# Merging weight bits in PSUM, and shorter chains of small operations, in an attention, memory and MLP kernel

## The chip, the cores and the metric

The kernel runs on one core of a Trainium2 chip. The time is what the device takes for one launch, in microseconds (us). The engines are TensorE (PE: matrix products and transposes, with PEld for its weight loads), VectorE (DVE), ScalarE (ACT), GpSimd (POOL) and SyncE (SP), whose queue starts the transfers (DMA). PSUM is the memory that PE writes to; SBUF is the large on-chip memory.

## The reference

Attention with a memory term over 4 batches, 8 heads, 576 positions of 64 values, then two matrix products over all 2304 tokens with a gate between them:

```python
scores = q @ k.T / sqrt(64), causal
a = exp(scores - max);  a /= a.sum(-1) + 1e-09;  local = a @ v
q_p = phi(q)                                  # max(q,0) + exp(min(q,0))
mem_out = (q_p @ M_prev) / ((q_p * z_prev).sum(-1) + 1e-6)
g = 1 / (1 + exp(-beta))                      # one value a head
x = g * mem_out + (1 - g) * local             # 2304 x 512
h = x @ w_in;  h = h / (1 + exp(-1.702 * h));  out = h @ w_out
```

`w_in` (512 x 2048) and `w_out` (2048 x 512) come as float64 and are used at float32 precision. Each float32 operand is used as a high and a low float32r part, and a product is the sum of three partial products.

## The kernel before

**Weights.** Both matrices are cut into 16 blocks of 128 x 512 values. A block arrives as pairs of 32-bit words (`wraw`, 512 KB). `conv_unit` makes float32 of it: ACT scales the upper words (L148), and DVE does three operations on bits in the SBUF tile `wr`: a shift (L153), the sign by and/or (L154), the low word by shift/or (L156). Then ACT copies the high part (`wi` or `wo`, L90), and POOL subtracts to get the low part (L100). Raw tiles: two buffers for `w_in`, three for `w_out`.

**Stages.** `first_queries` does the first 256 positions of batch 0 for all four head pairs. Then 16 (batch, head pair) units called pairs run through attention, one every 7 or 8 slots. `plan_prep` splits inputs into parts, computes phi(q) (`qm`, `qp`), its norm (`nrm`) and the memory matrix parts `ms`; `plan_attend` computes scores into PSUM tiles `ps`, maxima (L452), exponentials with sums (L458, `a` and `at`, sums in `sm` and `st`), inverses (L498 and L499, L526 and L528), scaling on POOL (L461), transposes (`pt`), their parts (`e`), and products with v into `po`. The result of a pair is `xf`, stored to DRAM (`xd`) and read back in chunks of x (`xl`, `xh`). The first matmul (`first_moe`, PSUM tiles `pm`, later `pm2`) runs over 8 chunks of tokens times 16 blocks and fills PE between attention work; its results `hk` go to DRAM (`gd`), copied out of PSUM by DVE and ACT in turn. The second stage reads them back (`graw`), gates them (`gt`, `gh`, `gl`) and multiplies by `w_out` (`acc`).

**The norm of the memory term.** The minimum of q with 0 is a DVE operation (L388), the exponential is ACT's (L392). DVE reduces over 64 values (L406), adds 1e-6 (L408), inverts (L409) and multiplies by the gate (L100, `nrm<-nrm,g`). `ms` is a copy (L93) and a subtraction (L100) of the memory matrix on DVE.

**What sets the order.** The program is written as events in slots; the framework then puts every engine's instructions into one list by its own schedule, which each engine follows. Pools hand out their buffers in the order of the program: a tile waits for the buffer's earlier tile, whatever the lists say. `ps_s` has five PSUM buffers under the tag "ps" for `ps` and `pt`; `ps_m2` has six for `pm2` in the late stage. In the program the 16 `w_in` conversions stand behind `first_queries` and ahead of all pairs; those of `w_out` are handed out one every two slots near the end of the first matmul.

Of the kernel before, what the change touches and what calls it, by code (L numbers as in the profile page):

```python
# [34 lines left out]
def tile_attention_memory_moe(ctx, tc, kq, vq, mem, zz, beta, w_in, w_out, out):  # L35
# [151 lines left out]
    def first_queries(b):  # L187
        K = []
# [50 lines left out]
        def phi():  # L239
            nc.vector.tensor_scalar(out=qm, in0=q, scalar1=0.0, scalar2=None, op0=ALU.min)  # L240
            nc.scalar.activation(out=qm, in_=qm, func=AF.Exp)
            nc.vector.scalar_tensor_tensor(out=q, in0=q, scalar=0.0, in1=qm, op0=ALU.max, op1=ALU.add)
            for c in range(NP):
                tt("P", qm[:, c], q[:, c], z[:, c:c + 1, :].to_broadcast([128, 2, 128]), ALU.mult)

        def phin():
            n = fst.tile([128, NP, 2, 2, 1], F32, name="fn")
            nc.vector.tensor_reduce(
                out=n[:, :, :, :, 0], in_=qm.rearrange("p c t (h d) -> p c t h d", h=2), op=ALU.add, axis=AX.X)
            nc.vector.tensor_scalar(out=n, in0=n, scalar1=1e-6, scalar2=None, op0=ALU.add)  # L250
# [1 line left out]
            for t in range(2):
                w = n[:, :, t, :, 0]
                tt("V", w, w, g.rearrange("p (c h) -> p c h", h=2), ALU.mult)
# [596 lines left out]
```

## Time and profile before

| | us |
|---|---|
| median of 3 runs | 706.65 (706.03 to 709.79) |
| the profiled execution | 706.16 |
| its span | 703.7 |

| engine | busy us in the span | share |
|---|---|---|
| PE | 632.4 | 90% |
| DVE | 493.9 | 70% |
| ACT | 393.4 | 56% |
| POOL | 292.3 | 42% |

The profiled execution lies within the runs; 2.5 us of its time lie outside the span. The mean granted clock of PE is 0.973. The shares are averages over stages that differ: conversions and the first pairs up to some 100 us, pairs with the first matmul to some 420 us, the end of the first matmul with the `w_out` conversions to 502.6 us, then the second matmul. So the profile is read by stretches of time, and in each by the chain of waits, which is followed back from the last instruction of the stretch to what released it. What stands in that chain ends last; a busy engine that is not in it can be shortened without effect.

### The profile page before, as it was taken

The numbers are of one execution on the slowest core, as the hardware profiler recorded it, in microseconds if no ns is written. First come the engines' busy times: TensorE is split into PE (matmuls) and PEld (weight loads), VectorE is DVE, ScalarE is ACT, GpSimd is POOL, SyncE is SP. The second block draws the span as 40 slices with busy tenths as digits, with TensorE's granted clock in tenths as the row PEclk, the third lists the DMA queues.
The fourth block names the chain that finished last, engine by engine and source line by source line (L and its number), as shares of the span: only waits on it lengthen the run. The fifth ranks groups of instructions, "written<-read, shape, count | busy, mean of one in ns | idle before, by whom it ended". The sixth has DMA issues, their size and how long they took to land.

```text
span 703.7 us, 12530 instructions
## 1 busy us (share of the span) xinstructions
PE 632.4 (90%) x3984; PEld 575.1 (82%) x3984; DVE 493.9 (70%) x1194; ACT 393.4 (56%) x951; POOL 292.3 (42%) x303
## 2 busy tenths in 40 slices
PE   3468887879998889999899999878999999999997
PEld 2256776669997789999899999778988888888897
DVE  4999998898778886687767635997255555555453
ACT  4467566686657764667576533543244545444453
POOL 4878766688447791665575203454000000000000
PEclk9989998999999999999999999999999999999999
DMA  8657858786677665766772128875233435335241
GB/s 257 181 193 198 243 153 227 197 234 170 174 203 195 187 196 174 198 173 175 231 195 82 44 85 308 277 214 186 83 90 105 150 104 152 100 101 151 69 128 53
DMA packets 71425, 116.70 MB, mean 166 GB/s; under 512 B 8768, under 2 KB 41024, under 8 KB 71360
## 3 DMA queue, kind: packets, MB, share of 16 engines
q1 hardware_dynamic: 71360, 115.91, 56.1%
q8 instruction: 32, 0.52, 0.3%
q14 instruction: 33, 0.27, 0.1%
HBM read 63.97 MB, written 27.79 MB: 130 GB/s over the span
## 4 chain that ended last, share of the span: by engine, by line
PE 62%; DVE 20%; DMA 7%; issue 4%; ACT 4%; SPq 1%; POOL 1%; DVEq 0%; ACTq 0%; POOLq 0%
PE acc L81 28%; PE pm L81 17%; PE po L81 6%; PE pt L85 5%; PE ps L81 4%; DVE wr L154 3%; DVE ps L452 3%; DVE wr L156 2%; DMA wraw<-in_w_in_dram 2%; DVE e L100 1%; DVE wr L153 1%; DMA gd<-hk 1%; DVE ms L93 1%; DMA graw<-gd 1%; DVE sm L498 1%
## 5 line engine op out<-in xcount | busy, mean ns | idle before, releaser
L81 PE MATMUL pm<-xh,wi 128*128 128x288 f32 (+2 forms) x1024 | 221.3, 306 | 13.4 <-ACT hk L90 7.1
L81 PEld LDWEIGHTS pm<-xh,wi 128*128 128x128 f32 x1024 | 168.9, 193 | 18.3 <-ACT hk L90 8.7
L81 PE MATMUL acc<-gh,wo 128*128 128x512 f32 (+1 forms) x640 | 179.7, 368 | 0.0
L81 PE MATMUL pm<-xl,wi 128*128 128x288 f32 (+2 forms) x512 | 153.7, 303 | 0.0
L81 PEld LDWEIGHTS acc<-gh,wo 128*128 128x128 f32 x640 | 115.2, 189 | 19.8
L81 PE MATMUL acc<-gl,wo 128*128 128x512 f32 (+1 forms) x320 | 115.5, 368 | 0.0
L461 POOL TENSOR_SCALAR a<-a,sm,g 128x512 f32<-128x512 f32 (+3 forms) x112 | 74.5, 677 | 59.6 <-DVE sm L499 32.8
L81 PEld LDWEIGHTS pm<-xl,wi 128*128 128x128 f32 x512 | 98.6, 193 | 0.3
L100 DVE TENSOR_TENSOR e<-pt,e 128x320 fp32r<-128x320 f32 (+2 forms) x152 | 69.5, 480 | 23.1 <-ACT e L90 22.4
L752 DVE SCALAR_TENSOR_TENSOR gt<-gt,graw 128x512 f32<-128x512 f32 (+1 forms) x80 | 52.1, 652 | 46.7 <-ACT gt L751 46.4
L100 DVE TENSOR_TENSOR gl<-gt,gh 128x512 fp32r<-128x512 f32 (+1 forms) x80 | 52.0, 650 | 46.0 <-ACT gh L90 42.9
L458 ACT ACTIVATE a<-ps,nm 128x512 f32<-128x512 f32 (+3 forms) x112 | 60.5, 542 | 36.8 <-DVE nm L452 34.1
L452 DVE CUSTOM_DVE_ANT_0 ps<-ps,mask 128x256 f32<-128x256 f32 (+4 forms) x144 | 69.3, 494 | 15.5 <-PE ps L81 10.9
L81 PE MATMUL po<-e,vs 128*128 128x320 f32 (+3 forms) x416 | 73.3, 295 | 4.1 <-DVE e L100 3.1
L90 ACT ACTIVATE e<-pt 128x320 fp32r<-128x320 f32 (+2 forms) x152 | 61.3, 433 | 27.3 <-PE pt L85 14.1
L751 ACT ACTIVATE gt<-graw 128x512 f32<-128x512 f32 (+1 forms) x80 | 47.1, 590 | 51.6 <-DVE gl L100 51.6
L90 ACT ACTIVATE gh<-gt 128x512 fp32r<-128x512 f32 (+1 forms) x80 | 47.1, 589 | 49.9 <-PE acc L81 46.6
L81 PEld LDWEIGHTS po<-e,vs 128*128 128x128 f32 x416 | 63.6, 195 | 6.1 <-DVE e L100 4.2
L81 PEld LDWEIGHTS acc<-gl,wo 128*128 128x128 f32 x320 | 59.4, 189 | 10.0
L81 PE MATMUL ps<-W 128*128 128x512 f32 (+3 forms) x224 | 59.1, 350 | 6.8 <-ACT at L458 1.8
L85 PE MATMUL pt<-ident,a 128*128 128x128 f32 x296 | 58.7, 282 | 1.4 <-ACT a L458 0.6
L85 PE MATMUL pt<-ident,at 128*128 128x128 f32 x160 | 43.0, 292 | 8.4 <-DVE e L100 5.0
(118 smaller groups left out, 1016.1 us busy)
## 6 DMA issues: line engine op xcount, KB each, us to landing
graw<-gd SPq DMA_DIRECT2D x64, 256.0 KB, 2.6
gd<-hk SPq DMA_DIRECT2D x96, 144.0 KB, 2.5
wraw<-in_w_in_dram SPq DMA_DIRECT2D x16, 512.0 KB, 4.0
wraw<-in_w_out_dram SPq DMA_DIRECT2D x16, 512.0 KB, 4.8
kqr<-in_kq_dram SPq DMA_DIRECT2D x12, 608.0 KB, 5.2
W<-hi SPq DMA_DIRECT2D x24, 272.0 KB, 4.0
W<-loq SPq DMA_DIRECT2D x48, 128.0 KB, 3.6
vr<-in_vq_dram SPq DMA_DIRECT2D x16, 320.0 KB, 4.0
```

What stands on the lines that cost most here:

```text
L81: nc.tensor.matmul(out, l, r, start=start, stop=stop)
L85: nc.tensor.transpose(out, in_, idn)
L90: nc.scalar.activation(out=dst, in_=src, func=AF.Copy, **kw)
L93: nc.vector.tensor_copy(dst, src)
L100: (nc.vector if eng == "V" else nc.gpsimd).tensor_tensor(out=dst, in0=a, in1=b, op=op)
L154: nc.vector.scalar_tensor_tensor(out=ri, in0=raw[:, :, 1], scalar=-2 ** 31, in1=ri, op0=ALU.bitwise_and, op1=ALU.bitwise_or)
L156: nc.vector.scalar_tensor_tensor(out=ri, in0=raw[:, :, 0], scalar=29, in1=ri, op0=ALU.logical_shift_right, op1=ALU.bitwise_or)
L452: nc.vector.tensor_tensor_reduce(out=ps, in0=ps, in1=mk, op0=ALU.add, op1=ALU.min, scale=-0.125, scalar=1e38 if j == 0 else nm[:, j - 1:j] ...
L458: nc.scalar.activation(out=a, in_=ps, func=AF.Exp, scale=-1.0, bias=nm, accum_out=sm)
L461: nc.gpsimd.tensor_scalar(out=a, in0=a, scalar1=r, scalar2=gcol, op0=ALU.mult, op1=ALU.mult)
L751: nc.scalar.activation(out=t[:, :n], in_=raw[:, :n], func=AF.Tanh, scale=0.851)
L752: nc.vector.scalar_tensor_tensor(out=t[:, :n], in0=t[:, :n], scalar=1.0, in1=raw[:, :n], op0=ALU.add, op1=ALU.mult)
```

## The change

1. **Bits in PSUM.** The scaled word goes into a PSUM tile `ws`, and the shift and the and/or work there; the third operation writes the SBUF tile `wr`. For `w_in` the tile takes a buffer of "ps", for `w_out` one of "pm2"; the last three `w_out` blocks, issued after that pool is closed, stay in SBUF.
2. **Small terms of denominators.** 1e-9 and 1e-6 stand in an additional column, set once by POOL; a reduction over the row takes the place of an addition. `qm` becomes one lasting tile `qmt` of width 65 for each head.
3. **Gate.** The memory matrix is multiplied by the gate when its parts are made: the high part by ACT with a scale, the low part by one DVE operation. The multiplication of the norm by the gate is gone.
4. **Minimum of q.** ACT computes Relu(-q), and the exponential takes its argument with scale -1.

```diff
-    def conv_unit(slot, dst, src, rp, rkw, sp, skw):
+    def conv_unit(slot, dst, src, rp, rkw, wp, wkw, sp, skw):
...
         def scale():
-            box["r"] = sp.tile([128, DM], F32, name="wr", **skw)
+            if wp() is None:
+                box["s"] = box["r"] = sp.tile([128, DM], F32, name="wr", **skw)
+            else:
+                box["s"] = wp().tile([128, DM], F32, name="ws", **wkw)
             nc.scalar.activation(
-                out=box["r"], in_=box["raw"][:, :, 1].bitcast(F32), func=AF.Copy, scale=2.0 ** -112)
+                out=box["s"], in_=box["raw"][:, :, 1].bitcast(F32), func=AF.Copy, scale=2.0 ** -112)
 
         def bits():
-            raw, ri = box["raw"], box["r"].bitcast(I32)
-            nc.vector.tensor_scalar(out=ri, in0=ri, scalar1=3, scalar2=None, op0=ALU.logical_shift_left)
+            raw, si = box["raw"], box["s"].bitcast(I32)
+            if "r" not in box:
+                box["r"] = sp.tile([128, DM], F32, name="wr", **skw)
+            nc.vector.tensor_scalar(out=si, in0=si, scalar1=3, scalar2=None, op0=ALU.logical_shift_left)
             nc.vector.scalar_tensor_tensor(
-                out=ri, in0=raw[:, :, 1], scalar=-2 ** 31, in1=ri, op0=ALU.bitwise_and, op1=ALU.bitwise_or)
+                out=si, in0=raw[:, :, 1], scalar=-2 ** 31, in1=si, op0=ALU.bitwise_and, op1=ALU.bitwise_or)
             nc.vector.scalar_tensor_tensor(
-                out=ri, in0=raw[:, :, 0], scalar=29, in1=ri, op0=ALU.logical_shift_right, op1=ALU.bitwise_or)
+                out=box["r"].bitcast(I32), in0=raw[:, :, 0], scalar=29, in1=si,
+                op0=ALU.logical_shift_right, op1=ALU.bitwise_or)
...
         def msplit():
-            copy("V", P["ms"][:, :, 0], raws[p]["m"])
-            sub("V", P["ms"][:, :, 1], raws[p]["m"], P["ms"][:, :, 0])
+            copy("A", P["ms"][:, :, 0], raws[p]["m"], gt[:, c:c + 1])
+            nc.vector.scalar_tensor_tensor(
+                out=P["ms"][:, :, 1], in0=raws[p]["m"], scalar=gt[:, c:c + 1], in1=f32(P["ms"][:, :, 0]),
+                op0=ALU.mult, op1=ALU.subtract)
...
         def qmin():
-            nc.vector.tensor_scalar(
-                out=P["qm"][:, T0:], in0=raws[p]["q"][:, T0:], scalar1=0.0, scalar2=None, op0=ALU.min)
+            nc.scalar.activation(out=qm, in_=qv(), func=AF.Relu, scale=-1.0)
...
         def norm():
-            nc.vector.tensor_reduce(
-                out=n[:, :, :, 0], in_=P["qm"][:, T0:].rearrange("p t (h d) -> p t h d", h=2), op=ALU.add, axis=AX.X)
-            nc.vector.tensor_scalar(out=n, in0=n, scalar1=1e-6, scalar2=None, op0=ALU.add)
+            nc.vector.tensor_reduce(out=n[:, :, :, 0], in_=qmt[:, T0:], op=ALU.add, axis=AX.X)
             nc.vector.reciprocal(out=n, in_=n)
-            tt("V", n[:, :, :, 0], n[:, :, :, 0],
-               g[:, None, 2 * c:2 * c + 2].to_broadcast([128, 5 - T0, 2]), ALU.mult)
...
         def inv_unit(i):
-            sm = U["sm", i]
-            nc.vector.tensor_scalar(out=sm, in0=sm, scalar1=1e-9, scalar2=None, op0=ALU.add)
+            sm = U["rs", i] = sml.tile([128, 2], F32, name="sm")
+            nc.vector.tensor_reduce(out=sm, in_=U["sm", i], op=ALU.add, axis=AX.X)
             nc.vector.reciprocal(out=sm, in_=sm)
...
     def conv_in(blk):
         wb[blk] = w1[blk >= W0].tile([128, 2, DM], F32R, name=f"wi{blk}")
-        conv_unit(None, wb[blk], w_in[blk], cnv, {"bufs": 2}, att, {"tag": f"qpt{blk % 2}", "bufs": 2})
+        conv_unit(None, wb[blk], w_in[blk], cnv, {"bufs": 2}, lambda: ps_s, {"tag": "ps"}, att, {"tag": f"qpt{blk % 2}", "bufs": 2})
...
-            conv_unit(state["slot"] + 1, wb[blk, 1], w_out[blk], wst2, {}, wst2, {})
+            conv_unit(state["slot"] + 1, wb[blk, 1], w_out[blk], wst2, {}, lambda: wide["ps"], {"tag": "pm2"}, wst2, {})
...
     for _ in range(3):
         conv_more()
         step()
+    wide["ps"] = None
     late.close()
```

The tail's sum and `first_queries` are changed in the same way as `inv_unit`, `norm`, `qmin` and `msplit`; in `first_queries` the memory matrix of four pairs is scaled by ACT.

The change also alters the order of the lists. A row shows the line, the operation, what it writes and reads, and its size; a number behind a name tells tiles of one name apart. DVE before, between the end of `first_queries` (`xl`) and the first two pairs, with one conversion (`wr_478`) in it:

```order
L153 TENSOR_SCALAR wr_478<-wr_478 128x512
L100 TENSOR_TENSOR xl_163<-po_379,xh_164 64x256
L396 SCALAR_TENSOR_TENSOR qp_936<-qr_788,qm_859 128x384
L498 TENSOR_SCALAR sm_843<-sm_843 128x2
L154 SCALAR_TENSOR_TENSOR wr_478<-wraw_476,wr_478 128x512
L452 ISA ps_969,nm_992<-ps_969,mask_118 128x288
L452 ISA nm_992 128x1
L100 TENSOR_TENSOR xl_163<-pm_385,xh_164 64x256
L499 RECIPROCAL sm_843<-sm_843 128x2
L156 SCALAR_TENSOR_TENSOR wr_478<-wraw_476,wr_478 128x512
```

DVE now, at the end of the `w_in` conversions (`ws_598` is the sixteenth block), where pair 0's first maximum (L475) stands:

```order
L170 SCALAR_TENSOR_TENSOR ws_576<-wraw_574,ws_576 128x512
L172 SCALAR_TENSOR_TENSOR wr_578<-wraw_574,ws_576 128x512
L169 TENSOR_SCALAR ws_587<-ws_587 128x512
L93 COPY hk_931<-pm_872 128x256
L170 SCALAR_TENSOR_TENSOR ws_587<-wraw_585,ws_587 128x512
L172 SCALAR_TENSOR_TENSOR wr_589<-wraw_585,ws_587 128x512
L169 TENSOR_SCALAR ws_598<-ws_598 128x512
L475 ISA ps_816,nm_853<-ps_816,mask_118 128x288
L475 ISA nm_853 128x1
L170 SCALAR_TENSOR_TENSOR ws_598<-wraw_596,ws_598 128x512
```

Before, a conversion has attention work of pairs 0 and 1 between its three operations; now fifteen blocks are through, with only `hk` copies and the last pieces of `first_queries` among them, when the first maximum of pair 0 comes.

SP's queue before, at loads of `w_in` (`wraw`) among those of the pairs' inputs:

```order
L143 DMA wraw_442<-in_w_in_dram 128x1024
L329 DMA qr_788<-in_vq_dram 128x384
L331 DMA zb_790<-in_zz_dram 128x128
L143 DMA wraw_456<-in_w_in_dram 128x1024
L326 DMA mr_986<-in_mem_dram 128x128
L324 DMA vr_984<-in_vq_dram 128x640
L143 DMA wraw_466<-in_w_in_dram 128x1024
```

And now, the same loads behind the inputs of the first pairs, from the third block on:

```order
L347 DMA mr_1031<-in_mem_dram 128x128
L345 DMA vr_1029<-in_vq_dram 128x640
L154 DMA wraw_449<-in_w_in_dram 128x1024
L154 DMA wraw_460<-in_w_in_dram 128x1024
L154 DMA wraw_471<-in_w_in_dram 128x1024
L154 DMA wraw_482<-in_w_in_dram 128x1024
L668 DMA gd0_97<-hk_642 128x256
L668 DMA gd1_98<-hk_665 128x256
L668 DMA gd2_99<-hk_668 128x256
L154 DMA wraw_497<-in_w_in_dram 128x1024
L668 DMA gd3_100<-hk_701 128x256
L154 DMA wraw_508<-in_w_in_dram 128x1024
```

The loads stood between loads of inputs; now each, from the seventh block on, stands behind the store of an earlier block's result of the first matmul.

DVE before, in the stretch with the `w_out` conversions, with the copies `hk` of the last chunks:

```order
L156 SCALAR_TENSOR_TENSOR wr_6889<-wraw_6820,wr_6889 128x512
L153 TENSOR_SCALAR wr_6957<-wr_6957 128x512
L154 SCALAR_TENSOR_TENSOR wr_6957<-wraw_6884,wr_6957 128x512
L93 COPY hk_6629<-pm_6588 128x288
L156 SCALAR_TENSOR_TENSOR wr_6957<-wraw_6884,wr_6957 128x512
L153 TENSOR_SCALAR wr_7021<-wr_7021 128x512
L154 SCALAR_TENSOR_TENSOR wr_7021<-wraw_6949,wr_7021 128x512
L156 SCALAR_TENSOR_TENSOR wr_7021<-wraw_6949,wr_7021 128x512
L93 COPY hk_6663<-pm_6619 128x288
```

And now, from the copy of the same block (`hk_6636`) on:

```order
L93 COPY hk_6636<-pm_6595 128x288
L93 COPY hk_6671<-pm_6626 128x288
L93 COPY hk_6704<-pm_6667 128x288
L93 COPY hk_6739<-pm2_6713 128x288
L93 COPY hk_6770<-pm2_6747 128x288
L169 TENSOR_SCALAR ws_6838<-ws_6838 128x512
L170 SCALAR_TENSOR_TENSOR ws_6838<-wraw_6765,ws_6838 128x512
L93 COPY hk_6832<-pm2_6788 128x288
L172 SCALAR_TENSOR_TENSOR wr_6840<-wraw_6765,ws_6838 128x512
L93 COPY hk_6867<-pm2_6819 128x288
```

Before, each copy has the three operations of a whole conversion between itself and the next; now copies stand together, and the remaining conversions come behind them, one for every two copies.

## Rows read from the trace of the kernel before

**Rows 1.** Busy time in six stretches: start:end length, busy (instructions), clock, DMA, GB/s

```profile
17.60:94.40 76.80, 55.09 (x330) 46.46 (x331) 72.92 (x149) 44.70 (x107) 60.73 (x54) 0.93 0.67 203
94.40:145.00 50.60, 40.84 (x247) 35.09 (x246) 45.52 (x138) 35.90 (x99) 34.63 (x33) 0.90 0.72 195
145.00:211.00 66.00, 62.02 (x445) 58.93 (x444) 55.14 (x165) 43.91 (x120) 42.28 (x46) 1.00 0.70 193
211.00:281.00 70.00, 60.83 (x422) 56.65 (x421) 56.64 (x176) 47.48 (x137) 46.01 (x50) 0.95 0.67 189
281.00:422.00 141.00, 138.50 (x1064) 137.27 (x1063) 97.22 (x305) 86.17 (x241) 68.19 (x79) 0.99 0.52 147
422.00:502.60 80.60, 71.33 (x499) 68.91 (x499) 56.42 (x78) 33.64 (x68) 32.76 (x24) 0.96 0.69 228
```

**Rows 2.** Chain of waits by line: 17.6:94.4, 94.4:145, 145:211, 211:281, 422:502.6 us

```profile
by line: DVE wr L154 18.8%; DMA wraw<-in_w_in_dram 13.8%; DVE wr L156 13.7%; DVE ps L452 8.0%; DVE wr L153 6.4%; issue 6.2%; ACT wr L148 3.4%; PE po L274 2.2%; DVE qm L388 2.0%; DVE ms L93 1.7%; PE pm L274 1.7%; PE po L275 1.7%; PE ps L81 1
...
by line: DVE ps L452 15.2%; issue 11.4%; PE pt L85 10.3%; PE po L81 10.0%; PE ps L81 6.4%; DVE e L100 5.9%; DVE ms L93 5.5%; DVE nrm L100 5.3%; DVE xf L100 4.5%; DVE qm L388 4.1%; DVE nrm L408 3.9%; DVE qpt L100 3.6%; DVE qp L396 3.5%; DVE 
...
by line: PE pm L81 15.4%; DMA gd<-hk 13.3%; PE po L81 6.4%; PE ps L81 6.2%; issue 6.0%; DVE ps L452 5.9%; PE pt L85 5.8%; DVE e L100 5.5%; DVE sm L498 5.1%; DVE ms L93 3.3%; ACT a L458 2.4%; POOL a L461 2.3%; ACT e L90 1.7%; ACT hi L90 1.7%
...
by line: PE pm L81 21.6%; PE po L81 9.5%; PE pt L85 9.0%; DMA xl<-xd 6.1%; PE ps L81 5.5%; DMA xd<-xf 5.4%; DVE e L100 5.3%; DVE ps L452 4.8%; issue 4.5%; ACT xh L90 3.2%; DVE sm L498 2.9%; DVE ms L93 2.2%; DVE qm L388 2.1%; ACT a L458 1.9%
...
by line: PE pm L81 31.7%; issue 15.3%; DVE wr L154 9.2%; DMA graw<-gd 8.5%; DMA wraw<-in_w_out_dram 6.2%; DVE wr L156 6.1%; DVE wr L153 5.3%; ACT wr L148 3.0%; SPq L143 2.8%; DVE hk L93 2.6%; DMA xd<-xf 2.6%; DVE gl L100 1.4%; SPq L645 1.3%
```

**Rows 3.** Tile `wr`: count, ns min/median/max, first and last start (us)

```profile
L153 DVE TENSOR_SCALAR wr<-wr x32: 386/416/1620, 16.8 to 483.0; 128x512 int32<-128x512 int32 x32
L154 DVE SCALAR_TENSOR_TENSOR wr<-wraw,wr x32: 672/693/2015, 17.4 to 483.7; 128x512 int32<-128x512 int32 x32
L156 DVE SCALAR_TENSOR_TENSOR wr<-wraw,wr x32: 673/1039/1699, 19.9 to 484.4; 128x512 int32<-128x512 int32 x32
```

**Rows 4.** Timeline, two places: start us, us, engine, line, operation

```profile
23.24 1.58 POOL L100 TENSOR_TENSOR vs<-vr,vs 128x640 fp32r<-128x640 f32 x1
...
23.36 2.02 DVE L154 SCALAR_TENSOR_TENSOR wr<-wraw,wr 128x512 int32<-128x512 int32 x1
...
45.30 0.69 DVE L154 SCALAR_TENSOR_TENSOR wr<-wraw,wr 128x512 int32<-128x512 int32 x1
```

**Rows 5.** Tile `e`; groups by form, line L95: busy us, mean ns

```profile
L100 DVE TENSOR_TENSOR e<-pt,e x152: 405/484/559, 76.0 to 413.3; 128x320 fp32r<-128x320 f32 x96, 128x256 fp32r<-128x256 f32 x32, 128x384 fp32r<-128x384 f32 x24
...
L95 DVE TENSOR_SCALAR ov<-acc 128x512 f32<-128x512 f32 x8 | 5.5, 686 | 0.4 <-PE acc L81 0.3
```

**Rows 6.** Operations on the tiles `sm` and `qm`

```profile
L498 DVE TENSOR_SCALAR sm<-sm x56: 101/169/3083, 59.1 to 399.0; 128x2 f32<-128x2 f32 x56
...
L388 DVE TENSOR_SCALAR qm<-qr x16: 341/489/1480, 25.6 to 351.6; 128x640 f32<-128x640 f32 x12, 128x384 f32<-128x384 f32 x4
L392 ACT ACTIVATE qm<-qm x16: 522/727/777, 26.7 to 353.0; 128x640 f32<-128x640 f32 x12, 128x384 f32<-128x384 f32 x4
...
L406 DVE TENSOR_REDUCE nrm<-qm x16: 537/814/822, 34.8 to 375.2; 128x10 f32<-128x640 f32 x12, 128x6 f32<-128x384 f32 x4
```

**Rows 7.** Busy time, 52.5 to 96.2 us: all; tile `wr` alone (DVE, ACT, POOL)

```profile
52.50:96.20 43.70, 37.18 (x251) 32.67 (x251) 41.93 (x88) 26.80 (x67) 32.25 (x26) 0.96 0.71 211
...
52.50:96.20 43.70, 25.64 (x27) 11.11 (x18) 13.82 (x10) 0.96 0.71 211
```

**Rows 8.** Tiles `xl`, `wi`, `xf`: first and last start of one operation each

```profile
L100 DVE TENSOR_TENSOR xl<-po,xh x4: 406/412/417, 43.3 to 58.3; 64x256 fp32r<-64x256 f32 x4
...
L90 ACT ACTIVATE wi<-wr x16: 612/629/632, 20.9 to 94.5; 128x512 fp32r<-128x512 f32 x16
...
L100 DVE TENSOR_TENSOR xf<-po,xb x56: 393/473/495, 96.2 to 421.6; 64x320 f32<-64x320 f32 x32, 64x256 f32<-64x256 f32 x24
```

**Rows 9.** Loads of raw `w_in` weights: DMA issues (page); chain of waits

```profile
wraw<-in_w_in_dram SPq DMA_DIRECT2D x16, 512.0 KB, 4.0
...
71.88 6.00 DMA wraw<-in_w_in_dram
```

More of the change, by code (lines that the diff above doesn't have):

```diff
@@ L70, in tile_attention_memory_moe @@
     events = {}
-    state = {"slot": -8, "pe": 0.0, "seq": 0}
+    state = {"slot": -8, "pe": 0.0, "seq": 0, "sum": 0}
     def at(slot, prio, fn):
@@ L124, in tile_attention_memory_moe @@
     g1t = cst.tile([128, NP], F32, name="g1t")
+    gt = cst.tile([128, NP], F32, name="gt")
+    sums = [sml.tile([128, 2, 2], F32, bufs=1, name=f"sum{k}") for k in range(8)]
+    tails = [sml.tile([128, 3], F32, bufs=1, name=f"tail{k}") for k in range(2)]
+    for t in sums:
+        nc.gpsimd.memset(t, 1e-9)
+    for t in tails:
+        nc.gpsimd.memset(t, 1e-9)
+    qmt = wkp.tile([128, 5, 2, D + 1], F32, name="qmt")
+    nc.gpsimd.memset(qmt, 1e-6)
     def gates():
@@ L203, in first_queries @@
         nc.sync.dma_start(m, mem[b * NP:b * NP + NP].rearrange("c p h d -> p c (h d)"))
-        qm = fst.tile([128, NP, 2, 128], F32, name="fqm")
+        qm = fst.tile([128, NP * 2, 2, D + 1], F32, name="fqm")
+        nc.gpsimd.memset(qm[:, :, :, D:], 1e-6)
+        for c in range(NP):
+            fs = fst.tile([128, 2, 2, 2], F32, name="fsm", bufs=NP)
+            nc.gpsimd.memset(fs, 1e-9)
+            fsm.append(fs)
         box = {}
-        sms, aa, fa = {}, {}, {}
+        aa, fa = {}, {}
         def score(c):
@@ L239, in phi @@
         def phi():
[L240 to L242 removed]
+            qv = q.rearrange("p c t (h d) -> p (c t) h d", h=2)
+            w = qm[:, :, :, :D]
+            nc.scalar.activation(out=w, in_=qv, func=AF.Relu, scale=-1.0)
+            nc.scalar.activation(out=w, in_=w, func=AF.Exp, scale=-1.0)
+            nc.vector.scalar_tensor_tensor(out=qv, in0=qv, scalar=0.0, in1=w, op0=ALU.max, op1=ALU.add)
             for c in range(NP):
[L244 removed]
+                tt("P", w[:, 2 * c:2 * c + 2], qv[:, 2 * c:2 * c + 2],
+                   z[:, c:c + 1, :].rearrange("p o (h d) -> p o h d", h=2).to_broadcast([128, 2, 2, D]), ALU.mult)
+                copy("A", m[:, c], m[:, c], gt[:, c:c + 1])
         def phin():
             n = fst.tile([128, NP, 2, 2, 1], F32, name="fn")
[L248 to L250 removed]
+            nv = n.rearrange("p c t h o -> p (c t) h o")
+            nc.vector.tensor_reduce(out=nv[:, :, :, 0], in_=qm, op=ALU.add, axis=AX.X)
             nc.vector.reciprocal(out=n, in_=n)
[L252 to L254 removed]
             for c in range(NP):
@@ L484, in exp_unit @@
             if h == 0:
-                U["sm", i] = sml.tile([128, 2], F32, name="sm")
+                state["sum"] = (state["sum"] + 1) % 8
+                U["sm", i] = sums[state["sum"]]
             if i == 3:
@@ L721, in tile_attention_memory_moe @@
     late = ExitStack()
-    moe_ps.append((pool(late, "ps_m2", 6, space=PSUM, side="right", reuse_waits="tile"), "pm2"))
+    ps_w = pool(late, "ps_m2", 6, space=PSUM, side="right", reuse_waits="tile")
+    moe_ps.append((ps_w, "pm2"))
+    wide = {"ps": ps_w}
     w2 = pool(ctx, "w2", side="right", reuse_waits="tile")
```

48 lines of the change are left out of this document (24 added, 24 removed).

## The prediction

> **What bounds the kernel now.** I read the profile by stages, first the busy time in each stretch [rows 1]. From 281 us to 422 us TensorE (PE) is busy 138.50 of 141.00 us: there the time is PE's, and what other engines save is worth nothing. The second matmul behind 502.6 us has no line that the change touches except the last three weight blocks, and I leave it as it is. Before 281 us PE is not full: VectorE (DVE) is busy 72.92 of 76.80 us up to 94.4 us and 45.52 of 50.60 us after it, while PE lies idle 21.7 and 9.8 us and its granted clock averages 0.93 and 0.90, between the levels of 1.2 and 2.4 GHz. From 145 to 281 us PE lacks 4.0 and 9.2 us, from 422 to 502.6 us it lacks 9.3 us at a clock of 0.96. These four stretches are what can be gained.
>
> Next, who ends last in them: the chain of waits, by line [rows 2]. Up to 94.4 us the three bit operations of the weight conversion (L153, L154, L156) are 38.9% of the chain and the loads of raw weights 13.8%. From 94.4 to 145 us L93 `ms`, L100 and L408 `nrm` and L388 `qm` hold 5.5+5.3+3.9+4.1 = 18.8%, 9.5 us. From 145 to 211 us `sm` L498 and `ms` hold 8.4%, 5.5 us; from 211 to 281 us `sm`, `ms` and `qm` 7.2%, 5.0 us. From 422 to 502.6 us the bit operations hold 20.6%, 16.6 us. All these lines are edited.
>
> **Why those operations are long.** The three bit operations have the same shape each time, but L153 lasts from 386 to 1620 ns, L154 from 672 to 2015 and L156 from 673 to 1699 [rows 3]. L154 took 2.02 us while GpSimd (POOL) was at a 1.58 us subtraction, and 0.69 us at 45.30 us, where POOL was idle [rows 4]. Operations of DVE with one input in PSUM do not stretch: 152 subtractions `e<-pt,e` lie between 405 and 559 ns over three widths, and a 128x512 scaling out of PSUM takes 686 ns [rows 5]. The same split holds for small ones: a 128x2 `sm` addition took up to 3083 ns, `qm` up to 1480, while the reduction of a 128x640 tile never took over 822 [rows 6].
>
> **Part 1, bits in PSUM.** From 52.5 to 96.2 us 27 bit operations, nine blocks, took 25.64 us of DVE [rows 7]: 2.85 us a block. With the scaled word in PSUM I price each of the three at 0.69 us, the value of the scaling out of PSUM [rows 5] and of the undisturbed L154 [rows 4]: 2.07 us. Ends: 1.8 us if the shift also keeps its undisturbed 0.39, its minimum [rows 3], and 3.15 us if the stretch stays and the shift loses 0.3. At 2.07 us, 0.78 us a block goes: 12.5 us over 16 `w_in` blocks, 10 us over the 13 `w_out` blocks that use PSUM.
>
> The shift shows what speaks against it: 386 ns at its best out of SBUF [rows 3], 686 ns for an operation of that width out of PSUM [rows 5]. The Trainium skill states the rule for that (VectorE: DVE Perf Modes, section Why PSUM operands drop a tier): any PSUM operand takes fp32 work down to the base rate. By the rule alone, with no relief of the stretch, 0.3 us times 29 blocks, 9 us of DVE, would be added; the rows on `e` say that the relief is larger.
>
> **Part 1 also moves work.** The new PSUM tiles take the score tiles' buffers in the order of the program, in which all 16 `w_in` blocks stand ahead of pair 0. The order shows it: before, conversions lie between the maxima, sums and norms of pairs 0 and 1; now all 16 run after the first queries, and pair 0's first maximum comes behind the shift of block 15. Every load of raw weights now also stands in SP's queue behind the store of the `hk` of an earlier block, so behind DVE, ACT and PE.
>
> When do they start? Before, the first queries' first `xl` came at 43.3 us [rows 8], behind five conversions, 5 x 2.85 = 14 us of DVE. Without them it comes at about 29 us, and the first shift, two places behind it in the order, at about 33.5 us, an estimate that leaves time for the scale, which ACT's list has behind `xh` copies of the first queries. The pace: two raw buffers, so two blocks need one load (4.0 us [rows 9]) plus the scale 0.63 (as the `wi` copy of the same width [rows 8]), bits 2.07 and a `hk` copy 0.4 (as the shortest of `e` [rows 5]), with 0.1 to issue: 7.2 us, 3.6 us a block, against (94.5-20.9)/15 = 4.9 us between `wi` copies now [rows 8]. Block 0 ends at 36 us, block 15 at 36 + 15 x 3.6 = 90 us, pair 0's first maximum at about 88. With a load of 6.00 us [rows 9] it would be 9.2 us a pair and an end at 105; with the loads hidden in part, 80.
>
> In before, pair 0's first maximum came at 52.5 us and its first finished piece `xf` at 96.2 [rows 8]. DVE was busy 41.93 us between them, 25.64 of it conversions [rows 7], so 16.3 us on the rest. Now only the rest is left: 88 + 16 = **104 us**, 8 us later than before. Bounds: 0 (end of conversions at 80) to 23 (end at 105).
>
> **Parts 2 to 4, small operations.** The gate multiplication goes; the added constants become part of a reduction, which does not stretch; `ms` high and the minimum of q go to ACT. ACT pays 0.73 us, its exponential of the same tile, for each minimum [rows 6], some 0.3 us for each copy: 16 us in all, on an engine busy 35.9 of 50.6 and 47.5 of 70 us [rows 1], where DVE is the busier. The low half of `ms` stays on DVE with two SBUF inputs and can still stretch. From the start of pair 0's output to 145 us, 9.5 us of chain goes; ACT comes second there, so I take **-7** (0 to -9.5). From 145 to 281 us 10.5 us of chain goes, but PE lacks only 13.2 us there, and the wait for the store and the load of x (5.4+6.1% of 70 us, 8 us, [rows 2]) stays: **-6** (-3 to -10.5).
>
> A row speaks against moving the minimum: on DVE its median is 489 ns, on ACT an operation of that size 727 [rows 6]. The Trainium skill's advice is the same (ScalarE: Activation LUTs, section Rules for kernel authors): relu, max and min belong on VectorE. By it, each move loses 0.24 us if ACT ended last, 16 x 0.24 = 4 us; in the chain [rows 2] the lines shown have DVE's `qm` and not ACT's.
>
> **The late conversions.** From 422 us, bits took 20.6% of 80.6 us of chain and go from 2.85 to 2.07 us a block. Before, conversion of one block stood next to that of the next, between the `hk` copies that free PE's buffers; now each takes a PSUM buffer in turn with PE's own tiles, and the order spreads them among the copies, the last three falling under the second matmul. PE lacks 9.3 us and 0.04 x 80.6 = 3.2 us by clock [rows 1]. I take **-7** (0, if PE now waits for a buffer that a conversion holds, to -12.5).
>
> **The sum.** The profiled execution took 706.16 us (703.7 in the span), the median is 706.65: half a microsecond, left out. 706.2 + 8 - 7 - 6 - 7 = 694.2, **694**. Ends: all bounds at their best 706.2 + 0 - 9.5 - 10.5 - 12.5 = 674; at their worst 706.2 + 23 - 0 - 3 - 0 = 726.
>
> **Rivals.** (a) Slower: the conversions in a row pace the start. If SP's queue holds each load for the store ahead of it, and loads take 6.0 us, a pair of blocks takes 10 us, block 15 ends at 111 us and pair 0's piece comes at 125: +29 - 20 = **715 us**. It decides from a loss of 20 us on, at 4.4 us a block, a load of 5.6 us. For it: the 6.00 us load in the chain, and two buffers only. Against: the median of 4.0 with the DMA queues as busy as they will be. (b) No change: what is saved is not on the path, since ACT or the DMA of x comes next, and the late start keeps its 8 us: -3 -3 -2 in place of -20, **706 us**. For it: chain terms of small operations overlap with one another. (c) Larger gain: conversions end at 80 us, no later start, and all chain terms come back in full: 706.2 - 30 = **676 us**. For it: DVE is the busy engine in every stretch where PE is not. (d) The change does not do what it says: bits stretch in PSUM too, 3.15 us a block; 8.3 us a pair, block 15 at 98 us, +16, the late stage gives nothing: 706.2 + 16 - 7 - 6 = **709 us**.
>
> **Chances.** Forecast (686 to 702) 0.45, (c) 0.20, (b) 0.13, (a) 0.15, (d) 0.07. A difference of 0.5%, 3.5 us, is about what a measurement of this kernel can tell from none. Faster by that: the forecast and (c) with a little of (b), 0.67; same: the rest of (b) and half of (d), 0.14; slower: (a) and half of (d), 0.19. The range goes from 676, case (c), to 713, short of (a)'s 715: what is left out is about 0.2.
>
> **What would show it.** Bit operations of 0.69 us with no spread; `wi` copies from 35 to 90 us every 3.6 us and no maxima among them; pair 0's first `xf` near 104 us; `sm` and `nrm` without stretched operations; PE's full stretch as long as before; PE lacking less than 5 us between the last attention pair and the second matmul. Wrong would be: a block over 4.4 us, an ACT that ends last between pair 0 and pair 8, or PE waiting for PSUM buffers while weights are converted.

## The result and the profile after

The changed kernel takes 700.71 us (698.03 to 702.07, 4 runs) beside 707.35 us of the kernel before (706.03 to 709.79): a ratio of 0.9898, with a 95% interval from 0.9856 to 0.9939. It is 1.0% faster. The forecast was 694 us, faster, in a range from 676 to 713. Ratios leave out executions that fell in a slower state of the chip (three of e11's ten, one of 17 of the kernel before beside e9 to e11), which the medians and ranges still hold.

The profiled execution took 702.07 us with a span of 700.3 us. The engines' busy time, from the page:

```profile
PE 636.1 (91%) x3984; PEld 575.9 (82%) x3984; DVE 442.2 (63%) x1128; ACT 407.6 (58%) x988; POOL 277.8 (40%) x319
```

DVE's busy time fell by 51.7 us from 493.9, ACT's grew by 14.2, POOL's fell by 14.5. The span is 3.4 us shorter in these two executions. Where it went, by the stretches of [rows 1], the last one cut at the start of the second matmul:

```profile
17.60:94.40 76.80, 54.70 (x278) 46.16 (x279) 48.63 (x105) 38.37 (x88) 37.40 (x39) 0.87 0.55 163
94.40:145.00 50.60, 40.63 (x260) 33.12 (x258) 40.41 (x134) 40.32 (x113) 38.93 (x41) 0.99 0.78 201
145.00:211.00 66.00, 62.49 (x426) 58.88 (x427) 48.23 (x159) 49.94 (x138) 45.90 (x50) 0.96 0.79 210
211.00:281.00 70.00, 59.29 (x404) 54.14 (x404) 49.06 (x154) 48.38 (x134) 45.69 (x50) 0.95 0.68 191
281.00:422.00 141.00, 141.00 (x1097) 139.77 (x1096) 96.96 (x307) 92.93 (x262) 71.18 (x82) 1.00 0.55 155
422.00:499.10 77.10, 72.26 (x540) 70.88 (x539) 41.66 (x71) 31.15 (x65) 21.80 (x19) 1.00 0.68 228
```

DVE is no longer full up to 94.4 us (48.63 of 76.80 in place of 72.92), and yet PE lacks as much as before there, 22.1 us, at a lower clock (0.87 in place of 0.93). PE lacks nothing from 281 to 422 us, and 4.8 us in place of 9.3 behind it.

The operations on bits, from the trace by tile (count, ns min/median/max, first and last start); the last row is the shift of the three `w_out` blocks that stay in SBUF:

```profile
L169 DVE TENSOR_SCALAR ws<-ws x29: 687/699/700, 35.6 to 496.1; 128x512 int32<-128x512 int32 x29
L170 DVE SCALAR_TENSOR_TENSOR ws<-wraw,ws x29: 678/695/733, 36.7 to 497.3; 128x512 int32<-128x512 int32 x29
L172 DVE SCALAR_TENSOR_TENSOR wr<-wraw,ws x29: 670/687/690, 37.9 to 498.9; 128x512 int32<-128x512 int32 x29
...
L169 DVE TENSOR_SCALAR wr<-wr x3: 422/424/1437, 499.5 to 506.9; 128x512 int32<-128x512 int32 x3
```

The stretch of [rows 3] is gone where a word is in PSUM: 670 to 733 ns for all 87 operations. The shift that stays in SBUF still reaches 1437 ns. The small operations, by tile:

```profile
L522 DVE TENSOR_REDUCE sm<-sum x56: 137/156/159, 95.2 to 405.8; 128x2 f32<-128x4 f32 x56
...
L415 ACT ACTIVATE qmt<-qr x16: 514/736/782, 21.8 to 360.3; 128x640 f32<-128x640 f32 x12, 128x384 f32<-128x384 f32 x4
...
L90 ACT ACTIVATE ms<-mr,gt x16: 389/420/437, 21.0 to 388.8; 128x128 fp32r<-128x128 f32 x16
L405 DVE SCALAR_TENSOR_TENSOR ms<-mr,gt,ms x16: 351/648/2428, 21.5 to 389.2; 128x128 fp32r<-128x128 f32 x16
```

The sum of `sm`, up to 3083 ns in [rows 6], now never takes over 159 ns. The low half of `ms`, with two inputs in SBUF, still stretches, to 2428 ns. The Trainium skill tells it so (SBUF — State Buffer, section Who interferes with whom): DVE and POOL share a pair of SBUF ports, which the one that issues first holds for a whole instruction; copies and operations with a scalar can ask for the pair, an operation with two SBUF inputs contends with POOL's reads, a reduction on trn2 never contends. The rows shown here agree (2428 and 1437 ns against 733 and 159).

When things happen, against [rows 8]: `wi` copies run from 38.7 to 94.4 us in place of 20.9 to 94.5, and `xf` from 107.2 to 428.4 in place of 96.2 to 421.6.

```profile
L90 ACT ACTIVATE wi<-wr x16: 614/631/640, 38.7 to 94.4; 128x512 fp32r<-128x512 f32 x16
...
L100 DVE TENSOR_TENSOR xf<-po,xb x56: 395/478/496, 107.2 to 428.4; 64x320 f32<-64x320 f32 x32, 64x256 f32<-64x256 f32 x24
```

So attention ends 6.8 us later than before, and the rest of the first matmul is 10 us shorter.

### The profile page after: what moved, and what is told of

Read it like the earlier page. It is cut to its first block, busy times and chain, and to the rows that moved or that the text cites. A ratio compares the mean times of both kernels' runs of the same rounds, so it can differ in the third digit from the quotient of the medians.

```text
span 700.3 us, 12529 instructions
## 1 busy us (share of the span) xinstructions
PE 636.1 (91%) x3984; PEld 575.9 (82%) x3984; DVE 442.2 (63%) x1128; ACT 407.6 (58%) x988; POOL 277.8 (40%) x319
## 4 chain that ended last, share of the span: by engine, by line
PE 70%; DMA 10%; ACT 7%; DVE 5%; issue 4%; POOL 3%; SPq 1%; ACTq 0%; DVEq 0%; POOLq 0%
PE acc L81 28%; PE pm L81 25%; PE po L81 6%; PE pt L85 5%; PE ps L81 5%; DMA xl<-xd 2%; DMA xd<-xf 2%; ACT a L481 2%; DMA wraw<-in_w_in_dram 1%; DMA fm<-in_mem_dram 1%; POOL wi L100 1%; DMA gd<-hk 1%; DMA kqr<-in_kq_dram 1%; ACT xh L90 1%; DVE ps L475 1%
## 5 line engine op out<-in xcount | busy, mean ns | idle before, releaser
L81 PE MATMUL pm<-xh,wi 128*128 128x288 f32 (+2 forms) x1024 | 224.8, 307 | 21.7 <-ACT wi L90 8.1
L484 POOL TENSOR_SCALAR a<-a,sm,g 128x512 f32<-128x512 f32 (+3 forms) x112 | 70.9, 644 | 57.1 <-DVE sm L523 40.2
L100 DVE TENSOR_TENSOR e<-pt,e 128x320 fp32r<-128x320 f32 (+2 forms) x152 | 70.5, 483 | 31.1 <-ACT e L90 29.7
L475 DVE CUSTOM_DVE_ANT_0 ps<-ps,mask 128x256 f32<-128x256 f32 (+4 forms) x144 | 69.7, 495 | 22.7 <-PE ps L81 12.2
L100 DVE TENSOR_TENSOR gl<-gt,gh 128x512 fp32r<-128x512 f32 (+1 forms) x80 | 53.9, 674 | 36.4 <-ACT gh L90 33.2
L85 PE MATMUL pt<-ident,a 128*128 128x128 f32 x296 | 56.8, 274 | 0.7 <-ACT a L481 0.4
L93 DVE COPY hk<-pm 128x288 f32<-128x288 f32 (+2 forms) x64 | 29.1, 455 | 43.3 <-PE pm L81 33.3
```

Source lines behind the costliest of these rows:

```text
L81: nc.tensor.matmul(out, l, r, start=start, stop=stop)
L85: nc.tensor.transpose(out, in_, idn)
L93: nc.vector.tensor_copy(dst, src)
L100: (nc.vector if eng == "V" else nc.gpsimd).tensor_tensor(out=dst, in0=a, in1=b, op=op)
L475: nc.vector.tensor_tensor_reduce(out=ps, in0=ps, in1=mk, op0=ALU.add, op1=ALU.min, scale=-0.125, scalar=1e38 if j == 0 else nm[:, j - 1:j] ...
L484: nc.gpsimd.tensor_scalar(out=a, in0=a, scalar1=r, scalar2=gcol, op0=ALU.mult, op1=ALU.mult)
```

## The experiments

**Theory A** is the prediction's: merging `w_in` in PSUM costs the start, because of the order; merging `w_out` in PSUM gains late; parts 2 to 4 gain in between. Rivals give the gain to one part alone. Three kernels, e1 to e3, tell them apart; with e4 they share the runs of the kernel before (707.63 us median in that group). Later groups have runs of their own of the kernel before (704.64 us for e5 to e8, 705.72 for e9 to e11, 705.38 for e12), so kernels of different groups are compared by their ratios. In each edit the framework makes the engines' lists anew, so a run prices an edit together with its order.

### e1: no bits in PSUM

```diff
-        conv_unit(None, ..., lambda: ps_s, {"tag": "ps"}, att, ...)
+        conv_unit(None, ..., lambda: None, {}, att, ...)
-            conv_unit(state["slot"] + 1, ..., lambda: wide["ps"], {"tag": "pm2"}, wst2, {})
+            conv_unit(state["slot"] + 1, ..., lambda: None, {}, wst2, {})
```

> The changed kernel with part 1 undone: all bits are merged in SBUF again, parts 2 to 4 stay. Theory A (part 1 costs the start and pays late): conversions and pairs 0 and 1 interleave again, pair 0's first xf at 92 to 96 us (107.2 in the changed kernel), bit operations stretch again to about 1 us on average, the small operations do not. The late stage from the last xf to the first acc is again about 80 us (70.7 in the changed kernel). Total about 702 us. Theory B (the whole gain is from parts 2 to 4, PSUM gives nothing in sum): at most 697 us. Theory C (the gain is from part 1 alone): 706 us or more.

Measured: 694.4 us, ratio 0.983 (0.9784 to 0.9876). Parts 2 to 4 alone give 1.7%, 12 us, more than the whole change, though the two intervals overlap a little: PSUM in sum costs, or gives nothing. This is theory B's number; theory A as put here was 8 us off. Its 702 us was not the prediction's sum, which without the two terms of part 1 is 706 - 7 - 6 = 693. Bit operations stretch again (L172 has a median of 1138 ns and a maximum of 1789), first `xf` at 94.7.

### e2 and e3: one of the two matrices

e2 takes only the second line of e1's edit (`w_in` in PSUM), e3 only the first (`w_out` in PSUM).

> The changed kernel with only the w_in bits in PSUM, the w_out bits back in SBUF. Theory A: the start stays late (first xf 107, last xf 428), and the late stage takes again about 80 us, so the total is 708 to 711 us. Theory D (the late stage is short because the late pairs left more of the first matmul done, not because of the w_out conversions): 700 to 702 us, late stage about 71 us.

Measured: 705.45 us, ratio 0.9984 (0.9956 to 1.0012), the late stage 77.5 us: nearer to A than to D, and 3 us below A's range.

> The changed kernel with only the w_out bits in PSUM, the w_in bits back in SBUF. Theory A: the start is as early as before or earlier (first xf 92 to 96, last xf 415 to 420), the late stage about 71 us, total 690 to 694 us, clearly faster than the changed kernel. Theory D: the late stage takes 78 us or more here, total 701 us or more.

Measured: 688.0 us, ratio 0.9752 (0.9697 to 0.9807), 2.5% faster than the kernel before and 1.5% faster than the change. Theory A holds, 2 us below its range, and D falls. In a table (the ratio to before; first and last `xf` and first `acc` from each profiled execution, us):

| `w_in` bits | `w_out` bits | ratio | first `xf` | last `xf` | first `acc` | last `xf` to `acc` |
|---|---|---|---|---|---|---|
| kernel before | | 1 | 96.2 | 421.6 | 502.3 | 80.7 |
| SBUF (e1) | SBUF | 0.983 | 94.7 | 414.3 | 490.4 | 76.1 |
| PSUM (e2) | SBUF | 0.9984 | 104.3 | 422.5 | 500.0 | 77.5 |
| SBUF (e3) | PSUM | 0.9752 | 96.0 | 413.0 | 483.5 | 70.5 |
| PSUM (the change) | PSUM | 0.9898 | 107.2 | 428.4 | 498.9 | 70.5 |

Down the columns: `w_in` in PSUM costs 1.5% with either place of `w_out` (0.9984 - 0.983, 0.9898 - 0.9752), 10 to 11 us. `w_out` in PSUM gains 0.8 to 0.9%, about 6 us, with either place of `w_in`; the intervals of e2 and the change are apart, those of e1 and e3 overlap. Whether the shorter operations bring it or the new order of the `hk` copies, no run separates. The parts add up.

What `w_in` in PSUM costs is PE's. Two stretches, up to 53 us and from there to 94.4 us, in the kernel before, in the change and in e3:

```profile
17.60:53.00 35.40, 20.05 (x91) 15.31 (x91) 33.07 (x69) 20.04 (x46) 29.52 (x29) 0.90 0.60 188
53.00:94.40 41.40, 35.04 (x241) 31.15 (x240) 39.85 (x83) 24.66 (x61) 31.21 (x25) 0.96 0.73 215
```

```profile
17.60:53.00 35.40, 26.95 (x130) 21.15 (x130) 21.74 (x55) 20.46 (x51) 20.89 (x26) 0.95 0.53 153
53.00:94.40 41.40, 27.75 (x150) 25.01 (x149) 26.89 (x51) 17.91 (x37) 16.51 (x13) 0.79 0.56 171
```

```profile
17.60:53.00 35.40, 23.30 (x95) 17.70 (x95) 32.54 (x63) 23.26 (x55) 31.64 (x31) 0.90 0.62 187
53.00:94.40 41.40, 34.71 (x230) 31.53 (x230) 35.60 (x76) 24.67 (x62) 27.82 (x24) 0.92 0.73 221
```

Up to 53 us the change is ahead: without conversions beside the first queries PE has 130 matmul records in place of 91 and 95. From 53 us on it falls behind, with 150 in place of 241 and 230, at a mean granted clock of 0.79, and no engine is full: DVE 26.89, ACT 17.91, POOL 16.51 of 41.40 us. PE's 13.65 us of idle there are all waits for a converted block, 8.1 us for ACT's high part and 5.6 for POOL's low part. Over both stretches PE lacks 22.1 us, in e3 18.8; of the first matmul it has done as much (204 records on `pm`, e3 196), so what is missing at 94.4 us is work of the pairs. Conversions in a row, with only the first chunk of the first matmul beside them, leave everybody waiting in turn. One turn, from the timeline of the change (an arrow names what ended the wait):

```profile
62.12 0.58 PE L81 MATMUL pm<-xh,wi 128*128 128x256 f32 x1 [0.99 <-POOL wi L100]
...
63.21 0.65 ACT L162 ACTIVATE ws<-wraw 128x512 f32<-128x512 f32 x1 [0.42 <-DMA wraw<-in_w_in_dram]
...
64.87 0.42 DVE L93 COPY hk<-pm 128x256 f32<-128x256 f32 x1 [0.27 <-PE pm L81]
...
65.21 0.69 DVE L170 SCALAR_TENSOR_TENSOR ws<-wraw,ws 128x512 int32<-128x512 int32 x1
...
66.00 0.69 DVE L172 SCALAR_TENSOR_TENSOR wr<-wraw,ws 128x512 int32<-128x512 int32 x1
...
66.79 0.33 SPq L154 DMA_DIRECT2D wraw<-in_w_in_dram  x1
```

PE waits for POOL's low part, DVE's `hk` copy waits for PE, the sign and the low word of the next block stand behind that copy on DVE, and the next load is issued when they are done.

Up to pair 0's first `xf` the change takes 11.2 us more than e3. PE lacks 5.2 us more of it (24.0 and 18.8 us from 17.6 us on), and for the other 6.0 it is busy longer, 65.6 us with 346 matmul records for 59.6 with 338. So about half of the loss is idle time and half is nearly the same matmuls taking longer, at the lower clock of the rows above (0.79 for 0.92); no run tests the clock by itself.

### e4 and e6: a PSUM buffer of its own, and what the fifth buffer is worth

```diff
-    ps_s = pool(attn, "ps_s", 5, space=PSUM, side="right")
+    ps_s = pool(attn, "ps_s", 4, space=PSUM, side="right")
+    ps_c = pool(attn, "ps_c", 1, space=PSUM, side="right")
...
-        conv_unit(None, ..., lambda: ps_s, {"tag": "ps"}, att, ...)
+        conv_unit(None, ..., lambda: ps_c, {"tag": "ws"}, att, ...)
```

> The changed kernel with the w_in words in a PSUM buffer of their own, and four buffers in place of five for scores and transposes. The order interleaves conversions with pairs 0 and 1 again. Theory A (the shared buffers in program order cost the start): first xf at 85 to 92 us, total 685 to 693 us. Rival (four buffers are too few for the pairs, or conversions in PSUM give nothing at the start): first xf at 96 or later, last xf 425 or later, total 698 us or more.

Measured: 718.74 us, ratio 1.0169 (1.0103 to 1.0234); first `xf` at 100.1, last at 449.3. The rival, but which half of it? e6 is e3 with only the first line of the edit:

> The kernel of e3 (w_in bits in SBUF, w_out bits in PSUM, 688.0 us) with four buffers for scores and transposes in place of five. If the fourth buffer alone explains why e4 (718.7 us) was slow: 705 to 720 us, last xf near 440 us. If the conversions in a buffer of their own were slow by themselves: 686 to 695 us, last xf near 415 us.

Measured: 710.92 us, ratio 1.0073 (1.0036 to 1.0110), last `xf` at 441.5. The fifth buffer of scores and transposes is worth 3.2% by itself (1.0073 - 0.9752), 23 us. From 281 to 410 us, first e6, then e3:

```profile
281.00:410.00 129.00, 121.77 (x912) 119.43 (x911) 86.64 (x267) 82.92 (x229) 67.61 (x76) 0.97 0.56 154
```

```profile
281.00:410.00 129.00, 128.72 (x1000) 127.44 (x999) 87.16 (x273) 82.85 (x233) 62.65 (x73) 1.00 0.55 156
```

With four buffers PE lacks 7.2 us where it lacked 0.3. e4 loses another 1.0% to e6, at the edge of the intervals: with four buffers for the scores, a buffer of its own for the words gains nothing. What it would do beside five is not tested.

### e5, e9 and e10: order, front and back

PSUM tiles come in the order of the program: behind the tiles of `first_queries` and ahead of pair 0. e5 hands the last ten conversions out in slots among pairs 0 and 1, which undoes the back:

```diff
-        conv_unit(None, wb[blk], ...)
+        conv_unit(None if blk < W0 else -7 + 2 * (blk - W0), wb[blk], ...)
...
+                while n == 0 and blk >= W0 and state["slot"] < -4 + 2 * (blk - W0):
+                    yield 1
                 ps = pp.tile([128, 512], F32, name=nm)
```

> The changed kernel (all bits but the last three blocks in PSUM) with the last ten w_in conversions handed out in slots among pairs 0 and 1, so that their PSUM tiles stand between the score tiles in the program and DVE's list mixes them. Theory A (the 12 us that w_in in PSUM costs come from the order, all conversions ahead of pair 0): pair 0's first xf back at 92 to 98 us, total 686 to 692 us, as with w_in in SBUF (688.0) or better. Theory E (they come from PSUM itself, five buffers shared by words and scores, or from how the loads are paced): total 696 us or more.

Measured: 696.48 us, ratio 0.9875 (0.983 to 0.9919). First `xf` came at 92.3, as theory A had it, but the total is theory E's: `wi` copies ran from 38.7 to 105.0, and the ratio cannot be told from the change's 0.9898. The front is undone by merging the first six blocks in SBUF: e9 is e5 with that, e10 the change with that.

```diff
-        ... lambda: ps_s, {"tag": "ps"}, att, ...)
+        ... lambda: None if blk < W0 else ps_s, {"tag": "ps"}, att, ...)
```

> The kernel of e5 (696.5 us: w_in words in PSUM, last ten blocks in slots) with the first six blocks merged in SBUF. Theory F (what e5 still loses is the front: PSUM tiles of the first blocks stand behind those of the first queries, so no conversion runs before 38 us): the first wi copy comes at 24 us again, six blocks are done by 48 us, first xf at 84 to 92 us, total 684 to 689 us. Rival (words in PSUM take buffers from the scores of pairs 0 and 1): first xf at 92 or later, total 693 us or more.

> The changed kernel (700.7 us) with the first six w_in blocks merged in SBUF, the other ten in PSUM still ahead of pair 0. Theory F (the front costs about 8 of the 12 us, the order ahead of pair 0 about 4): conversions from 24 to about 86 us, first xf at 98 to 101, total 691 to 694 us. Rival (only the place of pair 0 behind the last conversion counts and conversions are paced by the loads): total 698 us or more.

Measured: e9 690.44 us, ratio 0.9788 (0.9746 to 0.9831); e10 693.51 us, ratio 0.9832 (0.9793 to 0.9872). `wi` copies start at 24 us in both; in e10 they end at 81.9 us and the first `xf` comes at 97.6, both a little sooner than expected. e10 is where theory F had it, e9 between F and its rival. The front is worth 0.7% (e10 to the change) and 0.9% (e9 to e5), both at the edge of their intervals; the back 0.2 and 0.4%, inside them. As far as these runs tell, then, the larger part of what `w_in` in PSUM costs is that no conversion runs beside the first queries. That is likely and not shown, and how the rest divides stays open.

e9 shows something else. Its first `xf` comes 12 us before e3's (96.0), and it ends no sooner, 690.4 against 688.0 us:

```profile
L100 DVE TENSOR_TENSOR xf<-po,xb x56: 396/478/497, 84.1 to 414.8; 64x320 f32<-64x320 f32 x32, 64x256 f32<-64x256 f32 x24
```

Only pair 0 is early there: its store starts at 93.5 us for 100.9 in e3, that of pair 1 at 110.3 for 111.3. So an early pair 0 alone does not tell that the start was short.

### e11: stores out of the way of the loads

```diff
-            nc.sync.dma_start(gd[blk][:, t0:t0 + w], h[:, :w])
+            (nc.scalar if n == 0 else nc.sync).dma_start(gd[blk][:, t0:t0 + w], h[:, :w])
```

> The changed kernel (700.7 us) with the 16 stores of the first chunk's hk issued from ACT's queue in place of SP's, so that no load of raw weights stands behind a store. Theory G (loads wait in SP's queue for stores, which wait for the first matmul at a low clock): a block every 3.2 to 3.4 us in place of 3.72, last wi copy at 86 to 90 us in place of 94.4, total 692 to 697 us. Rival (two raw buffers, load and bits set the pace by themselves): a block every 3.6 us or more, total 699 us or more.

Measured: 708.49 us, ratio 1.0022 (0.9987 to 1.0056). The copies ran from 37.9 to 92.2 us, (92.2 - 37.9)/15 = 3.6 us a block:

```profile
L90 ACT ACTIVATE wi<-wr x16: 612/629/637, 37.9 to 92.2; 128x512 fp32r<-128x512 f32 x16
```

Theory G falls: the stores in SP's queue are not what paces the conversions. That two raw buffers, a load, the bits and the copy behind them do is read off the turn shown above, and a pace of 3.6 to 3.7 us is that of the prediction's sum; no run with a third raw buffer tests it. Why the whole kernel loses 1.2% against the change with stores on ACT's queue is not settled: the loss comes behind 145 us, where PE lacks 6.7 of 66.0 us in place of 3.5.

### e7, e8 and e12: parts 4, 2 and 3, each undone in e3

```diff
-            nc.scalar.activation(out=qm, in_=qv(), func=AF.Relu, scale=-1.0)
+            nc.vector.tensor_scalar(out=qm, in0=qv(), scalar1=0.0, scalar2=None, op0=ALU.min)
```

> The kernel of e3 (688.0 us) with the minimum of q of the 16 pairs back on DVE (part 4 undone there). Theory A (DVE was the engine that ended last, ACT has room): 2 to 5 us slower, 690 to 693 us. Rival (ACT is what ends last now, and each Relu costs it 0.74 us): 2 to 5 us faster, 683 to 686 us.

Measured: 692.66 us, ratio 0.9822 (0.9784 to 0.9861), in theory A's range.

```diff
-            nc.vector.tensor_reduce(out=sm, in_=U["sm", i], op=ALU.add, axis=AX.X)
+            nc.vector.tensor_scalar(out=sm, in0=U["sm", i][:, :, 0], scalar1=1e-9, scalar2=None, op0=ALU.add)
```

and the same for `st` and `nrm`:

> The kernel of e3 (688.0 us) with part 2 undone in the pairs: the additions of 1e-9 and 1e-6 on sm, st and nrm are operations of DVE again. Theory A (operations that stretch beside POOL sit in the chain): sm additions last up to 3 us again, total 3 to 7 us slower, 691 to 695 us. Rival (they were only waiting for what came next anyway): 687 to 689 us.

Measured: 695.54 us, ratio 0.985 (0.9817 to 0.9884), just above theory A's range; the rival falls. The addition, on the same two elements, in e8:

```profile
L523 DVE TENSOR_SCALAR sm<-sum x56: 152/170/2061, 56.5 to 396.4; 128x2 f32<-128x2 f32 x56
...
361.47 2.06 DVE L523 TENSOR_SCALAR sm<-sum 128x2 f32<-128x2 f32 x1
...
361.94 1.57 POOL L100 TENSOR_TENSOR vs<-vr,vs 128x640 fp32r<-128x640 f32 x1
```

The longest of them ends at 363.53 us, as POOL's subtraction does (363.51).

```diff
-            copy("A", P["ms"][:, :, 0], raws[p]["m"], gt[:, c:c + 1])
-            nc.vector.scalar_tensor_tensor(out=P["ms"][:, :, 1], in0=raws[p]["m"], scalar=gt[:, c:c + 1], ...)
+            copy("V", P["ms"][:, :, 0], raws[p]["m"])
+            sub("V", P["ms"][:, :, 1], raws[p]["m"], P["ms"][:, :, 0])
...
+            tt("V", n[:, :, :, 0], n[:, :, :, 0], g[...].to_broadcast([128, 5 - T0, 2]), ALU.mult)
```

> The kernel of e3 (688.0 us) with part 3 undone in the pairs: ms is a copy and a subtraction on DVE again, the gate multiplies the norm on DVE. If the three small parts add up to the 13 us that parts 2 to 4 bring together (e7 costs 4.7, e8 7.5): 689 to 692 us. If each of them alone is covered in part by the others: 694 us or more, since the parts undone one at a time then sum to more than 13.

Measured: 694.41 us, ratio 0.9846 (0.9792 to 0.99); the copy of `ms` on DVE reached 1534 ns again. Undone one at a time from e3 they cost 0.7, 1.0 and 0.9% (0.9822, 0.985 and 0.9846 less 0.9752), 2.6% in sum, where together they brought 1.7% to the kernel before. Of the three only e8's interval lies clear of e3's; those of e7 and e12 overlap it. That the sum is beyond 1.7%, as the second case of e12 has it, is therefore a hint and not shown.

## Why the prediction was right, step by step

Each of the three terms has the sign that was forecast, and the runs give each its size (by ratios, times 707 us):

| term | predicted | measured | from |
|---|---|---|---|
| late start of attention | +8 | +10 to +11 | e1 to e2, e3 to the change |
| small operations, 94 to 281 us | -7 and -6 | -12 | before to e1 |
| late conversions | -7 | -6 | e1 to e3, e2 to the change |

The measured terms come to 10.5 - 12 - 6 = -7.5 us, which is what the change gave (its ratio of 0.9898 is 7.2 us). The forecast was -12, so a little over half of it came. Of what is missing, 2 to 3 us are the start's, about 1 us is missing in each of the other two.

**The price of an operation in PSUM** was put at 0.69 us; it is 0.67 to 0.73. Rival (d), bits that stretch in PSUM too, falls with the first rows after. The shift takes 0.42 us in SBUF undisturbed and 0.70 us in PSUM. The rule weighed there agrees, though it is stated for fp32 and the shift works on int32 (the Trainium skill, VectorE: DVE Perf Modes, section Why PSUM operands drop a tier). The loss of 0.28 us is real, and the stretch that goes is larger.

**The start** is the term that was mis-sized, +8 for +10 to +11. The first queries' `xl` began at 33.6 us where I had 29, the first shift at 35.6 for 33.5, the `wi` copies ran from 38.7 to 94.4 us, 3.7 us a block, where I had blocks done from 36 to 90 at 3.6; `xf` followed at 107.2 for 104. That is 11 us behind the kernel before, and 3 us more than forecast. The measure that I took, pair 0's first result, held here: against e3 its first `xf` is 11.2 us late and its last one 15.4. It is luck in part, since e9 shows that it need not hold. What it stands for is PE: from 53 to 94.4 us PE lacked 13.65 us in place of 6.4, at a clock of 0.79 in place of 0.96. The stretch ahead of it had given 6.9 us of idle back.

**Parts 2 to 4** gave what was predicted in sum, 12 us for 13, but not where. By the time of the store of pair 8 (started at 257.6 us in e1 and 261.4 before) 3.8 us were gained, by the last pair's (414.8 and 422.0) 7.2, by the first `acc` 11.9. I had written that from 281 us on other engines' savings are worth nothing. Savings made earlier do come back there, as e1 shows (from 422 us to its first `acc`):

```profile
422.00:490.50 68.50, 60.97 (x431) 58.50 (x430) 54.00 (x74) 33.49 (x66) 35.37 (x24) 0.98 0.75 244
```

PE is busy 61.0 us there where it was busy 71.3 [rows 1], and lacks 7.5 us for 9.3. No edited line of parts 2 to 4 stands in this stretch. Most of the difference is that e1's pairs were over 7.3 us sooner: from its last `xf` at 414.3 to 422 us PE was busy without a gap (7.70 of 7.70 us). Counted from the last `xf` to the first `acc`, e1 has 490 matmul records left and the kernel before 502, 3.0 us of PE's busy time, and PE lacks 1.7 us less. So of the 11.9 us some 7.3 came by the end of the pairs, 3.0 as work of the first matmul done earlier, in gaps between the pairs' work, and 1.7 as less idle time behind them.

**Minimum of q on ACT.** The rule against it (VectorE for minima, in the Trainium skill's ScalarE: Activation LUTs, section Rules for kernel authors) would have had e7 faster. It is 0.7% slower, with intervals that overlap, so no gain from DVE is shown, nor a loss beyond doubt. On ACT the operation takes 736 ns in the median and 549 on DVE in e7, but there it reaches 1490. ACT is in the chain from 94.4 to 145 us now, though, where DVE's small operations were [rows 2]:

```profile
by line: issue 14.0%; DMA kqr<-in_kq_dram 12.6%; ACT a L481 11.6%; DMA qr<-in_vq_dram 8.7%; DMA xd<-xf 7.9%; ACT e L90 6.9%; PE ps L81 4.1%; DVE ps L475 3.9%; SPq L392 3.6%; ACT xb L90 3.2%; PE pm L81 2.8%; ACT qmt L415 2.4%; DVE ms L405 2.
```

Loads of inputs and ACT's exponentials stand first in it, and DVE's lines have become small. An ACT that ends last was one of the prediction's signs of being wrong; its lines shown here hold 24.1%, so the sign is there in part up to 145 us.

**The late stage** went as told: no new wait on PSUM buffers. The chain from 422 us to the first `acc` is PE's:

```profile
by line: PE pm L81 78.9%; DMA xl<-xd 8.3%; issue 3.4%; ACT xh L90 1.9%; PE po L81 1.7%; DVE gl L100 1.0%; DVE ws L169 0.9%; DVE wr L172 0.9%; ACT ws L162 0.7%; ACT wo L90 0.7%; DVE hk L93 0.6%; SPq L668 0.5%; DVE gt L777 0.4%; SPq L154 0.2%
```

The bit operations held 20.6% of it before [rows 2].

**The rivals.** (a) was right that conversions in a row pace the start, and wrong on its price: a block took 3.7 us, not 5, and e11 shows that the stores in SP's queue are not the cause. (b) falls with e1 and e3, (c) with the first `xf`, which came later than before. The fastest kernel measured is e3, the change without its PSUM tiles for `w_in`: 688.0 us.
